# A chunked recurrence with two expert layers: products in pairs of 64 weight columns, and more tiles for px and s0

## The chip, the cores and the metric

The kernel runs on one core of a Trainium2 chip. The metric is device time in microseconds (us) of one execution. In the rows, PE is TensorE's matmuls, PEld its weight loads, DVE VectorE, ACT ScalarE, POOL GpSimd, SP the engine whose queue issues the DMAs. TensorE's clock is granted at one of two levels, 1.2 or 2.4 GHz; the rows give it as a share of 2.4 GHz (0.50 or 1.00, between them a mean over time).

## What is computed

A recurrence over 768 steps for 32 heads (4 batches of 8) with a 40x40 state, then two expert layers on its output:

```
for t in range(S):
    y[:, :, t] = einsum('bhd,bhde->bhe', rt, state)
    Sa = einsum('bhde,bhe->bhd', state, at)
    state = state * wt[:, :, None, :] - einsum('bhd,bhe->bhde', Sa, bt) + einsum('bhd,bhe->bhde', vt, kt)
x = y as (B, S, 320)
x = x + (u * (w_sg @ norm(v) + b_sg)) @ w_out       # u, v = halves of gelu(x @ w_in)
out = (h * sigmoid(conv3(h))) @ w_out2              # h = relu(x @ w_in2)
```

Inputs and outputs are float32.

## The kernel before

**Stages.** `attention` takes the 768 steps in 12 chunks of 64 (`hg`), two chunks to a group (`g`, 6 groups). The 32 heads lie as 16 pairs (`P` is the head of a pair: rows or columns 0 to 63 and 64 to 127); a half `q` of a chunk holds 8 pairs. Then `moe` runs the two layers. The recurrence takes the first 690 us or so, the layers the rest.

**A chunk's work.** `prep` loads the decays and `a`, `k`, `b`, runs two scans on VectorE (`px` and `w`), multiplies `at` by `px` and `kbt` by `w`, and squares `px` and `w` on ScalarE for a guard (`junk`). `products` makes `gk` (L127), masks it into `la`, and transposes `kbt` by TensorE (`pkb`, L133) into `kbn`. `kbt` has one tile, so the next chunk's load waits for the transpositions of this one; `px` and `kbn` have four tiles each, `at` four. `solve_a` inverts a group's triangular blocks on VectorE (60 small operations, L170 and L172, on `mu`); `solve_b` finishes them with 32x32 products (`pn`, `pt`; `n1` shares its tile with `mu`). `chain` is the recurrence proper: `py` (L230), copied to `ys`; `pz` (L237), copied to `vz`; `pS` (L246, L249), the new state, scaled by `px` (L254) and copied to `st`; and, off that path, `pzt` (L258), copied to `zv`. `spart` transposes the state into `s0` (three tiles). `ypart` makes `gh` (L282), masks it into `ghs`, sums `pyo` (L291, L293), multiplies by `px` into `xo` (L296) and stores `xo` with four DMAs.

**Shapes on TensorE.** `a*b` in a row is the part of the array in use: rows times weight columns. Every float32 product is two records in the trace; a transposition by `nc.tensor.transpose` is one. `py`, `pS`, `p0` and `pyo` use 128 rows and 64 weight columns, and two heads of a pair stand in the two halves of the columns; `pz` uses 64*64; `pzt`, `gk`, `gh` and `pkb` 128*128; `pn` and `pt` 32*32.

**What sets the order.** The groups' steps are recorded by the list `ORDER` with priorities (`level`). The framework then fixes each engine's order once, when the program is built, from those priorities, from its own estimates of durations, and from when tiles come free. So a tile more, or a product of another shape, moves instructions on every engine. At run time each engine works through its fixed order and waits where an operand or a tile isn't ready.

Of the kernel before, what the change touches and what calls it, by code (L numbers as in the profile page):

```python
# [10 lines left out]
F32 = mybir.dt.float32  # L11
F16 = mybir.dt.float16
# [3 lines left out]
AF = mybir.ActivationFunctionType  # L16
# [11 lines left out]
def _attention(ctx, tc, ident, gu, wp, wr, a, kb, r, vt, v, x):  # L28
# [5 lines left out]
    nc = tc.nc  # L34
    D, C, J = 40, 64, 4
# [5 lines left out]
    ps_a = ctx.enter_context(tc.tile_pool(name="ps_a", bufs=2, space=PSUM))  # L41
# [24 lines left out]
    las = [const.tile([128, 2, 8, J, C], F32, name=f"la_{i}") for i in range(2)]  # L66
    rys = ring("ys_", 2, [128, 8, 2, C], 0.0, nc.gpsimd)
    rst = ring("st_", 2, [128, 8 * D + 24], 0.0, nc.gpsimd, 8 * D)
    rs0 = ring("s0_", 3, [128, 8 * D + 24], 0.0, nc.gpsimd, 8 * D)
    real = [slice(64 * P, 64 * P + D) for P in range(2)]  # L70
    rq = lambda q: slice(32 * q, 32 * q + 32)
    heads = [(i, P) for i in range(8) for P in range(2)]
    m8 = mask[:, None, None, :].to_broadcast([128, J, 2, C])

    tl, grp = {}, {}

    def flat(t):
        return t.rearrange("p n t -> p (n t)")

    def prep(hg):  # L80

        at = e2.tile([128, 16, 2, C], F32, name="at", bufs=4)
        kbt = e1.tile([128, 16, 2, C], F32, name="kbt")
        px = p4.tile([128, 16, 65], F32, name="px")
        ws = [[], []]
        for q in range(2):
            for i, src in enumerate((wp, wr)):
                t = e2.tile([128, 8, 65], F32, name=f"w{i}")
                nc.sync.dma_start(out=flat(t), in_=src[hg, :, 520 * q:520 * q + 520])
                ws[q].append(t)  # L90
            if q == 0:
                nc.sync.dma_start(out=at.rearrange("p n P t -> p (n P t)"), in_=a[hg])
                nc.sync.dma_start(out=kbt.rearrange("p n c t -> p (n c t)"), in_=kb[hg])
        for q in range(2):
            ns = slice(8 * q, 8 * q + 8)
            w1, w2 = ws[q]
            nc.vector.memset(first[:, :, 0], 1.0)
            nc.vector.tensor_tensor_scan(out=flat(px[:, ns]), data0=flat(w1), data1=flat(first), initial=0.0,
                                         op0=ALU.mult, op1=ALU.add)
            nc.vector.reciprocal(first[:, :, 0], px[:, ns, 64])  # L100
            nc.vector.tensor_tensor_scan(out=flat(w2), data0=flat(w2), data1=flat(first), initial=0.0,
                                         op0=ALU.mult, op1=ALU.add)
            nc.vector.tensor_tensor(out=at[:, ns], in0=at[:, ns], in1=px[:, ns, None, 0:C].to_broadcast([128, 8, 2, C]),
                                    op=ALU.mult)
            nc.vector.tensor_tensor(out=kbt[:, ns], in0=kbt[:, ns],  # L105
                                    in1=w2[:, :, C - 1::-1][:, :, None, :].to_broadcast([128, 8, 2, C]), op=ALU.mult)
            for i, t in enumerate((flat(px[:, ns]), flat(w2))):
                junk = e1.tile([128, 8 * 65], F16, name="junk")
                u = 4 * hg + 2 * q + i
                nc.scalar.activation(out=junk, in_=t, func=AF.Square, scale=2.0 ** -32, accum_out=gu[:, u:u + 1])  # L110
        tl[hg] = dict(px=px, at=at, kbt=kbt)

    def products(hg):

        g, tq = divmod(hg, 2)
        if tq == 0:
            grp[g] = dict(la=las[g % 2])
        la = grp[g]["la"]
        d = tl[hg]
        at, kbt = d["at"], d["kbt"]  # L120
        kbn = p4.tile([128, 32 * D + 24], F32, name="kbn")
        nc.gpsimd.memset(kbn[:, 32 * D:], 0.0)  # L122
        for c in range(4):
            pg = ps_g.tile([128, J, 2, C], F32, name="gk", tag="pg")
            for j in range(J):
                n = 4 * c + j
                nc.tensor.matmul(out=pg[:, j].rearrange("p P t -> p (P t)"),  # L127
                                 lhsT=kbt[:, n].rearrange("p c t -> p (c t)"),
                                 rhs=at[:, n].rearrange("p P t -> p (P t)"), start=True, stop=True)
            nc.vector.tensor_tensor(out=la[:, :, 4 * tq + c].rearrange("p P j t -> p j P t"), in0=pg, in1=m8, op=ALU.mult)  # L130
            pa = ps_a.tile([128, 4, 128], F32, name="pkb", tag="pa")
            for j in range(J):
                nc.tensor.transpose(out=pa[:, j], in_=kbt[:, 4 * c + j].rearrange("p c t -> p (c t)"), identity=ident)  # L133
            nc.scalar.activation(out=kbn[:, 8 * D * c:8 * D * c + 8 * D].rearrange("p (m e) -> p m e", e=D),
                                 in_=pa.rearrange("p j (P e) -> p (j P) e", P=2)[:, :, 0:D], func=AF.Copy)
        cs = slice(4 * tq, 4 * tq + 4)
        for P in range(2):
            rows = rq(2 * P + 1)
            nc.scalar.activation(out=la[rows, P, cs, :, 0:32], in_=la[rows, P, cs, :, 32:64], func=AF.Copy)
        d.update(kbn=kbn)  # L140
# [42 lines left out]
    def solve_b(g, tq):  # L183
# [4 lines left out]
        for c in range(4):  # L188
            for j in range(J):
                for P in range(2):  # L190
                    nc.tensor.matmul(out=pn[rq(2 * P + 1), c, j], lhsT=la[rq(2 * P), P, 4 * tq + c, j, 32:64],
                                     rhs=tn[rq(2 * P), 4 * tq + c, j], start=True, stop=True,
                                     tile_position=(64 * P, 64 * P + 32))
        n1 = e1.tile([128, 4, J, 32], F32, name="n1", tag="mu")
        for P in range(2):
            i1 = rq(2 * P + 1)
            nc.scalar.activation(out=n1[i1], in_=pn[i1], func=AF.Copy)
# [23 lines left out]
    def chain(g, c4):  # L221
# [10 lines left out]
        ys = rys(q)  # L232
# [1 line left out]
            nc.scalar.activation(out=ys[half[P], :, P, 0:D], in_=py[half[P]], func=AF.Copy)  # L234
        pz = ps_c.tile([128, 8, D], F32, name="pz", tag="pc")
        for i, P in heads:
            nc.tensor.matmul(out=pz[half[P], i], lhsT=tt[half[P], 2 * c4 + i // 4, i % 4],  # L237
                             rhs=ys[half[P], i, P, 0:D], start=True, stop=True)
        nc.vector.tensor_copy(vz[half[0], 0, q], pz[half[0]])  # L239
        nc.scalar.activation(out=vz[half[1], 1, q], in_=pz[half[1]], func=AF.Copy)  # L240
        if hg < NH - 1:
# [32 lines left out]
    def ypart(g, c4):  # L274
# [531 lines left out]
```

## Time and profile before

| what | us |
|---|---|
| median of 3 runs (lowest, highest) | 1193.69 (1191.77, 1199.42) |
| the profiled execution | 1188.77 |
| its span, first to last instruction | 1187.1 |
| TensorE busy in the span | 944.4 |
| VectorE busy in the span | 707.7 |

All views are of the one profiled execution. A group of instructions has a busy time (the union of its spans) and the mean length of one record; records of TensorE overlap, so the busy time divided by the count is what one costs in a stream, and the mean length is not. "Idle before" is the time that the engine stood idle just ahead of them, with what ended most of it.

### The profile page before, as it was taken

How to read it: one execution, taken by the hardware profiler on the slowest of the kernel's cores; microseconds unless marked ns; L12 is line 12 of the kernel's file. 1: busy time of each engine (PE TensorE's matmuls, PEld its weight loads, DVE VectorE, ACT ScalarE, POOL GpSimd, SP SyncE). 2: the span in 40 equal slices, each digit the busy share in tenths (PEclk: the TensorE clock that was granted, in tenths of full speed). 3: DMA queues.
4: the chain of work that ended last, by engine and by line, in shares of the span. 5: the costliest groups of instructions: out<-in, count | busy, mean ns of one | idle time of the engine just before them, and what ended most of it. 6: DMA issues, size and time to landing. Idle time of an engine off the chain costs nothing.

```text
span 1187.1 us, 23136 instructions
## 1 busy us (share of the span) xinstructions
PE 944.4 (80%) x9777; PEld 871.2 (73%) x9777; DVE 707.7 (60%) x1325; ACT 468.4 (39%) x913; POOL 145.4 (12%) x164
## 2 busy tenths in 40 slices
PE   3225965797888889789978756899999977999895
PEld 3225864686877778778867745799999966999894
DVE  5693289169692767559233342865556668677763
ACT  2214432433522442352234132423222346777772
POOL 2000000000000000000001012211111424333331
PEclk9655786598766876875876878899999988999997
DMA  9512155225512522420251182000000221000000
GB/s 317 185 36 72 57 174 154 73 84 156 165 60 70 171 104 83 150 64 13 74 177 36 54 240 60 30 1 1 1 1 1 85 60 34 29 23 17 18 23 31
DMA packets 47489, 94.48 MB, mean 80 GB/s; under 512 B 20240, under 2 KB 26384, under 8 KB 44304
## 3 DMA queue, kind: packets, MB, share of 16 engines
q1 hardware_dynamic: 47376, 92.91, 24.8%
q8 instruction: 79, 1.29, 0.5%
q14 instruction: 34, 0.28, 0.1%
HBM read 85.02 MB, written 7.86 MB: 78 GB/s over the span
## 4 chain that ended last, share of the span: by engine, by line
PE 45%; DVE 26%; DMA 8%; ACT 7%; issue 5%; POOL 3%; SPq 1%; DVEq 0%; POOLq 0%; ACTq 0%
PE pv L615 6%; PE pzt L258 4%; DVE mu L172 4%; DVE mtmp L170 4%; PE pr L636 4%; PE gh L282 3%; PE ph L566 3%; PE gk L127 3%; PE pq L706 3%; PE pu L597 3%; DMA raw<-in_moe_w_in 2%; PE pz L237 2%; PE py L230 2%; DMA raw<-in_moe_w_out 2%; DVE mu L163 2%
## 5 line engine op out<-in xcount | busy, mean ns | idle before, releaser
L127 PE MATMUL gk<-at,kbt 128*128 128x128 f32 x384 | 71.5, 353 | 83.9 <-DVE kbt L105 50.5
L127 PEld LDWEIGHTS gk<-at,kbt 128*128 128x128 f32 x384 | 65.3, 260 | 87.1 <-DVE kbt L105 49.5
L692 POOL TENSOR_TENSOR cv<-cv,hz 128x384 f32<-128x384 f32 x64 | 62.4, 984 | 124.2 <-ACT cv L691 124.2
L282 PE MATMUL gh<-r,zv 128*128 128x128 f32 x384 | 72.3, 328 | 1.8 <-DMA r<-in_c_r 1.8
L258 PE MATMUL pzt<-tt,ys 128*128 128x64 f32 x384 | 66.9, 345 | 2.5 <-DVE vz L254 2.5
L258 PEld LDWEIGHTS pzt<-tt,ys 128*128 128x128 f32 x384 | 62.7, 255 | 8.2 <-issue 7.0
L293 PE MATMUL pyo<-ghs,kbn 128*64 128x64 f32 x768 | 60.7, 234 | 7.8 <-DVE ghs L286 7.6
L615 PE MATMUL pv<-sg_hi,vh 128*128 128x384 f32 x192 | 64.5, 336 | 1.2 <-ACT vh L589 1.2
L282 PEld LDWEIGHTS gh<-r,zv 128*128 128x128 f32 x384 | 57.7, 222 | 9.4 <-issue 3.7
L291 PE MATMUL pyo<-r,s 128*64 128x64 f32 x704 | 63.1, 241 | 1.7 <-DVE xo L296 1.7
L615 PE MATMUL pv<-sg_lo,vh 128*128 128x384 f32 x192 | 64.4, 336 | 0.0
L286 DVE TENSOR_TENSOR ghs<-gh,mask 128x512 f32<-128x512 f32 x48 | 32.4, 687 | 52.5 <-PE pyo L293 38.7
L615 PE MATMUL pv<-sg_hi,vl 128*128 128x384 f32 x192 | 63.6, 336 | 0.0
L293 PEld LDWEIGHTS pyo<-ghs,kbn 128*64 128x64 f32 x768 | 52.6, 146 | 14.4 <-DVE ghs L286 9.6
L172 DVE TENSOR_TENSOR mu<-mu,mtmp 128x30 f32<-128x30 f32 (+9 forms) x180 | 59.4, 330 | 5.1
L170 DVE TENSOR_TENSOR mtmp<-mu 128x30 f32<-128x30 f32 (+9 forms) x180 | 59.0, 328 | 5.4
L122 POOL MEMSET kbn<- 128x24 f32 x12 | 1.2, 118 | 497.8 <-PE pyo L293 497.8
L706 PE MATMUL pq<-wv_hi,gh 128*128 128x320 f32 x192 | 43.2, 331 | 22.7 <-ACT gh L695 22.7
L696 DVE TENSOR_TENSOR gl<-cv,gh 128x384 fp32r<-128x384 f32 x64 | 40.9, 640 | 31.8 <-ACT gh L695 31.7
L239 DVE COPY vz<-pz 64x320 f32<-64x320 f32 x24 | 11.6, 481 | 81.0 <-PE pz L237 80.8
L291 PEld LDWEIGHTS pyo<-r,s 128*64 128x64 f32 x704 | 52.2, 147 | 6.4 <-issue 2.8
L230 PE MATMUL py<-vz,la 128*64 128x40 f32 (+1 forms) x768 | 45.6, 290 | 11.8 <-ACT la L209 4.3
(149 smaller groups left out, 2384.7 us busy)
## 6 DMA issues: line engine op xcount, KB each, us to landing
at<-in_c_a SPq DMA_DIRECT2D x12, 1024.0 KB
kbt<-in_c_kb SPq DMA_DIRECT2D x12, 1024.0 KB
zv<-in_c_vt SPq DMA_DIRECT2D x24, 512.0 KB
r<-in_c_r SPq DMA_DIRECT2D x24, 512.0 KB
w<-in_c_wp SPq DMA_DIRECT2D x24, 260.0 KB
w<-in_c_wr SPq DMA_DIRECT2D x24, 260.0 KB
raw<-in_moe_w_in SPq DMA_DIRECT2D x8, 512.0 KB
vz<-in_c_v SPq DMA_DIRECT2D x24, 160.0 KB
```

The source lines that it names most:

```text
L127: nc.tensor.matmul(out=pg[:, j].rearrange("p P t -> p (P t)"), lhsT=kbt[:, n].rearrange("p c t -> p (c t)"), rhs=at[:, n].rearrange("p P t ...
L170: nc.vector.tensor_tensor(out=tv, in0=mu[:, j + 1:32, j:j + 1].to_broadcast([128, n, j]), in1=mu[:, j:j + 1, 0:j].to_broadcast([128, n, j] ...
L172: nc.vector.tensor_tensor(out=mu[:, j + 1:32, 0:j], in0=mu[:, j + 1:32, 0:j], in1=tv, op=ALU.subtract)
L230: nc.tensor.matmul(out=py[half[P], i], lhsT=la[rows, P, 2 * c4 + i // 4, i % 4], rhs=vz[rows, P, q, i], start=True, stop=True)
L258: nc.tensor.matmul(out=pzt[:, i], lhsT=ys[:, i].rearrange("p P e -> p (P e)"), rhs=tt[:, 2 * c4 + i // 4, i % 4], start=True, stop=True)
L282: nc.tensor.matmul(out=gh[:, j].rearrange("p P t -> p (P t)"), lhsT=zv[:, 4 * s + j].rearrange("p c t -> p (c t)"), rhs=r2[:, 4 * s + j].r ...
L291: nc.tensor.matmul(out=pyo[half[P], i], lhsT=s0s[hg, q][:, D * i:D * i + 64], rhs=r2[:, i, P], start=True, stop=False)
L293: nc.tensor.matmul(out=pyo[half[P], i], lhsT=rows_of(kbn, q, i, P), rhs=ghs[:, j, P], start=(hg == 0), stop=True)
L615: nc.tensor.matmul(out=po, lhsT=l[:, fs], rhs=rr[:, k, cs], start=(n == 0), stop=(n == 3 * NT - 1))
L636: nc.tensor.matmul(out=po, lhsT=ww[:, k, ms], rhs=ghl[k][i], start=(n == 0), stop=(n == 3 * NF1 - 1))
L692: nc.gpsimd.tensor_tensor(out=cv, in0=cv, in1=h[:, 1:N2 + 1], op=ALU.mult)
L706: nc.tensor.matmul(out=po, lhsT=gs[k][g][:, ts], rhs=rr[:, k], start=(n == 0), stop=(n == 3 * NF2 - 1))
```

## The change

`pzt` becomes 16 products with 64 weight columns and 128 rows, in the order of the heads, where there were 8 with 128 weight columns; `pz` reads all 128 rows of `tt` and `ys` (the other head's rows of `ys` are zero); `kbn`'s transposition becomes pairs of ordinary products with `kbt` as weights (64 columns) and 80 columns of the identity. `px` gets five tiles, `s0` four; `n1` gets a tile of its own beside `mu`; `ghs` and `xo` share three tiles (they had two each); the squares write into the spent `w` tile and `junk` goes.

```
-    rs0 = ring("s0_", 3, [128, 8 * D + 24], 0.0, nc.gpsimd, 8 * D)
+    rs0 = ring("s0_", 4, [128, 8 * D + 24], 0.0, nc.gpsimd, 8 * D)
+    id80 = ident.rearrange("p (P e) -> p P e", P=2)[:, :, 0:D]
-        px = p4.tile([128, 16, 65], F32, name="px")
+        px = p4.tile([128, 16, 65], F32, name="px", bufs=5)
-                junk = e1.tile([128, 8 * 65], F16, name="junk")
-                nc.scalar.activation(out=junk, in_=t, func=AF.Square, scale=2.0 ** -32, accum_out=gu[:, u:u + 1])
+                nc.scalar.activation(out=flat(w1), in_=t, func=AF.Square, scale=2.0 ** -32, accum_out=gu[:, u:u + 1])
-            pa = ps_a.tile([128, 4, 128], F32, name="pkb", tag="pa")
+            pa = ps_a.tile([128, J, 2, D], F32, name="pkb", tag="pa")
             for j in range(J):
-                nc.tensor.transpose(out=pa[:, j], in_=kbt[:, 4 * c + j].rearrange("p c t -> p (c t)"), identity=ident)
+                for h in range(2):
+                    nc.tensor.matmul(out=pa[half[h], j], lhsT=kbt[:, 4 * c + j, h], rhs=id80, start=True, stop=True)
-        n1 = e1.tile([128, 4, J, 32], F32, name="n1", tag="mu")
+        n1 = e1.tile([128, 4, J, 32], F32, name="n1")
         for i, P in heads:
-            nc.tensor.matmul(out=pz[half[P], i], lhsT=tt[half[P], 2 * c4 + i // 4, i % 4],
-                             rhs=ys[half[P], i, P, 0:D], start=True, stop=True)
+            nc.tensor.matmul(out=pz[half[P], i], lhsT=tt[:, 2 * c4 + i // 4, i % 4],
+                             rhs=ys[:, i, P, 0:D], start=True, stop=True)
-        for i in range(8):
-            nc.tensor.matmul(out=pzt[:, i], lhsT=ys[:, i].rearrange("p P e -> p (P e)"),
-                             rhs=tt[:, 2 * c4 + i // 4, i % 4], start=True, stop=True)
+        for i, P in heads:
+            nc.tensor.matmul(out=pzt[half[P], i], lhsT=ys[:, i, P], rhs=tt[:, 2 * c4 + i // 4, i % 4],
+                             start=True, stop=True)
-            ghs = p2.tile([128, J, 2, C], F32, name="ghs")
+            ghs = p3.tile([128, J, 2, C], F32, name="ghs", tag="gx")
-        xo = p2.tile([128, 2, J, C], F32, name="xo")
+        xo = p3.tile([128, 2, J, C], F32, name="xo", tag="gx")
```

VectorE, where a group ends (the solve of the next one is done, `ypart` stores its results): this is the order before, in group 3.

```order
L296 TENSOR_TENSOR xo<-pyo,px 128x512 x2
L98 SCALAR_TENSOR_TENSOR px<-w_2961,first 128x520
L100 RECIPROCAL first<-px 128x8
L103 TENSOR_TENSOR at<-at,px 128x1024
L101 SCALAR_TENSOR_TENSOR w_2963<-w_2963,first 128x520
L105 TENSOR_TENSOR kbt<-kbt,w_2963 128x1024
L97 MEMSET first 128x8
```

VectorE with the change, at the start of a group, just after the next solve's first transpositions:

```order
L297 TENSOR_TENSOR xo<-pyo,px 128x512
L164 STREAM_TRANSPOSE mu<-la_103 64x1024 x2
L99 SCALAR_TENSOR_TENSOR px<-w_4175,first 128x520
L171 TENSOR_TENSOR mtmp<-mu 128x30
L101 RECIPROCAL first<-px 128x8
L104 TENSOR_TENSOR at<-at,px 128x1024
```

The scan of `px` now stands inside the solve. VectorE with the change, at the end of that group, for the same chunk:

```order
L179 STREAM_TRANSPOSE tt_99<-mu 128x32x32
L287 TENSOR_TENSOR ghs<-gh,mask 128x512
L240 COPY vz<-pz 64x320
L106 TENSOR_TENSOR kbt<-kbt,w_4177 128x1024
L106 TENSOR_TENSOR kbt<-kbt,w_4183 128x1024
```

The scans, the reciprocals and the multiplications of `at` moved some 75 rows ahead, into the solve; of the chain behind `xo` only the multiplications of `kbt` are left at the group's end.

TensorE, in a pair of `chain` steps, before (the number behind a name is a buffer's):

```order
L237 MATMUL pz<-ys_105,tt_100 64x40 x15
L258 MATMUL pzt<-tt_100,ys_105 128x64 x8
L133 MATMUL pkb<-ident,kbt 128x128 x4
L203 MATMUL pt<-tt_100,n_3505 32x32
L249 MATMUL pS<-vz,kbn 64x40
L230 MATMUL py<-vz,la_104 64x40 x16
L249 MATMUL pS<-vz,kbn 64x40 x15
L133 MATMUL pkb<-ident,kbt 128x128 x2
L237 MATMUL pz<-ys_106,tt_100 64x40
```

TensorE at the same place with the change:

```order
L238 MATMUL pz<-ys_105,tt_99 64x40 x16
L247 MATMUL pS<-st_109,ident 64x320 x2
L259 MATMUL pzt<-tt_99,ys_105 64x64 x13
L250 MATMUL pS<-vz,kbn 64x40
L259 MATMUL pzt<-tt_99,ys_105 64x64 x3
L134 MATMUL pkb<-ident,kbt 64x80 x2
L231 MATMUL py<-vz,la_103 64x40 x16
L250 MATMUL pS<-vz,kbn 64x40 x15
L134 MATMUL pkb<-ident,kbt 64x80 x5
```

All rows here are of one array shape, where four alternated; `pzt` and `pkb` stand in smaller pieces between the others. Over TensorE's whole order the array's shape changes 306 times with the change, 331 times before.

VectorE in the first solve (`run(solve_a(0))`), before:

```order
L172 TENSOR_TENSOR mu<-mu,mtmp 128x26x5
L170 TENSOR_TENSOR mtmp<-mu 128x150
L172 TENSOR_TENSOR mu<-mu,mtmp 128x25x6
L170 TENSOR_TENSOR mtmp<-mu 128x168
L172 TENSOR_TENSOR mu<-mu,mtmp 128x24x7
```

VectorE at the same place with the change, where the fifth `px` tile is first used:

```order
L171 TENSOR_TENSOR mtmp<-mu 128x150
L99 SCALAR_TENSOR_TENSOR px<-w_1067,first 128x520
L173 TENSOR_TENSOR mu<-mu,mtmp 128x25x6
L101 RECIPROCAL first<-px 128x8
L171 TENSOR_TENSOR mtmp<-mu 128x168
```

A scan and a reciprocal of the fifth chunk now stand inside the first solve.

## Rows read from the trace of the kernel before

**Rows 1.** Windows by stage: prologue, recurrence, layers; columns stand in its first line.

```profile
core 0: us, PE busy (x) PEld busy (x) DVE busy (x) ACT busy (x) POOL busy (x), PEclk, DMA share, GB/s
0.00:100.00 100.00, 25.54 (x224) 23.97 (x224) 71.30 (x125) 21.70 (x51) 7.56 (x22) 0.70 0.48 160
100.00:690.00 590.00, 482.08 (x7152) 430.92 (x7152) 332.54 (x627) 211.38 (x404) 9.20 (x14) 0.73 0.33 103
690.00:1187.10 497.10, 436.79 (x2401) 416.29 (x2401) 303.90 (x573) 235.32 (x460) 128.62 (x128) 0.94 0.12 36
```

**Rows 2.** TensorE's waits, 100 to 690 us: total, times, longest.

```profile
PE gk L127 <- DVE first L97: 19.8, 3, 7.6
PE pt L203 <- ACT n L197: 16.6, 13, 4.7
PE gk L127 <- issue: 13.2, 2, 7.0
PE pyo L293 <- DVE ghs L286: 7.6, 9, 3.5
...
PE gk L127 <- DVE kbt L105: 5.4, 5, 2.7
PE pS L249 <- DVE vz L239: 4.8, 5, 1.6
```

**Rows 3.** Timeline of VectorE ahead of one such wait: start, us, operation, idle.

```profile
382.27 1.29 DVE L296 TENSOR_TENSOR xo<-pyo,px 128x512 f32<-128x512 f32 x2 [3.76 <-PE pyo L293]
383.59 1.24 DVE L98 TENSOR_TENSOR_SCAN px<-w,first 128x520 f32<-128x520 f32 x1
384.87 0.21 DVE L100 RECIPROCAL first<-px 128x8 f32<-128x8 f32 x1
384.99 1.18 DVE L103 TENSOR_TENSOR at<-at,px 128x1024 f32<-128x1024 f32 x1
386.08 1.23 DVE L101 TENSOR_TENSOR_SCAN w<-w,first 128x520 f32<-128x520 f32 x1
387.35 1.22 DVE L105 TENSOR_TENSOR kbt<-kbt,w 128x1024 f32<-128x1024 f32 x1
```

**Rows 4.** Timeline of TensorE at the end of it.

```profile
388.63 2.08 PE L127 MATMUL gk<-at,kbt 128*128 128x128 f32 x8 [6.05 <-DVE first L97]
```

**Rows 5.** Groups by shape, 100 to 690 us: array*columns, count, busy, mean ns, idle.

```profile
L258 PE MATMUL pzt<-tt,ys 128*128 128x64 f32 x384 | 66.9, 345 | 2.5 <-DVE vz L254 2.5
L291 PE MATMUL pyo<-r,s 128*64 128x64 f32 x704 | 63.1, 241 | 1.7 <-DVE xo L296 1.7
L293 PE MATMUL pyo<-ghs,kbn 128*64 128x64 f32 x768 | 60.7, 234 | 7.8 <-DVE ghs L286 7.6
L293 PEld LDWEIGHTS pyo<-ghs,kbn 128*64 128x64 f32 x768 | 52.6, 146 | 14.4 <-DVE ghs L286 9.6 <-issue 1.4 <-DVE mu L172 0.2
L237 PE MATMUL pz<-ys,tt 64*64 64x40 f32 x768 | 43.8, 270 | 0.4 <-ACT ys L234 0.4
L230 PE MATMUL py<-vz,la 128*64 128x40 f32 x704 | 42.3, 293 | 10.7 <-ACT la L209 4.3 <-DVE first L100 3.4 <-ACT vz L240 3.1
```

**Rows 6.** The same view over the whole span, transpositions.

```profile
L133 PE MATMUL pkb<-ident,kbt 128*128 128x128 f32 x192 | 40.8, 344 | 0.8 <-ACT kbn L134 0.8
```

**Rows 7.** Timeline, runs of one product at 1.2 GHz: pzt, pkb, py.

```profile
426.45 3.67 PE L258 MATMUL pzt<-tt,ys 128*128 128x64 f32 x16
429.92 1.06 PE L133 MATMUL pkb<-ident,kbt 128*128 128x128 f32 x4
...
362.87 1.88 PE L230 MATMUL py<-vz,la 128*64 128x40 f32 x32
```

**Rows 8.** Timeline, runs of one product at 2.4 GHz: pkb, gh, pyo, pzt, py.

```profile
154.51 0.60 PE L133 MATMUL pkb<-ident,kbt 128*128 128x128 f32 x4
154.94 1.95 PE L282 MATMUL gh<-r,zv 128*128 128x128 f32 x16
156.82 0.69 PE L293 MATMUL pyo<-ghs,kbn 128*64 128x64 f32 x16
160.00 1.38 PE L293 MATMUL pyo<-ghs,kbn 128*64 128x64 f32 x32 [1.41 <-DVE ghs L286]
...
239.89 2.00 PE L258 MATMUL pzt<-tt,ys 128*128 128x64 f32 x16
...
470.52 1.13 PE L230 MATMUL py<-vz,la 128*64 128x40 f32 x32
```

**Rows 9.** Timeline, shapes alternating at 2.4 GHz.

```profile
501.10 0.33 PE L291 MATMUL pyo<-r,s 128*64 128x64 f32 x2
501.36 0.49 PE L282 MATMUL gh<-r,zv 128*128 128x128 f32 x2
501.78 0.33 PE L293 MATMUL pyo<-ghs,kbn 128*64 128x64 f32 x2
```

**Rows 10.** Windows: one with gk, gh and pkb, one mixed, two of chain steps.

```profile
148.00:162.00 14.00, 11.80 (x165) 11.13 (x167) 10.02 (x14) 4.68 (x11) 0.00 (x0) 1.00 0.56 189
236.00:274.00 38.00, 34.59 (x666) 30.50 (x664) 27.09 (x62) 14.79 (x31) 0.12 (x1) 0.99 0.33 107
333.00:353.00 20.00, 18.70 (x195) 16.34 (x196) 18.45 (x48) 4.50 (x10) 0.00 (x0) 0.50 0.21 70
357.00:377.00 20.00, 20.00 (x218) 17.46 (x216) 2.84 (x5) 3.41 (x7) 0.00 (x0) 0.50 0.09 28
```

**Rows 11.** Chain of waits, two DMAs: start, us, what.

```profile
140.05 4.70 DMA kbt<-in_c_kb
269.26 4.24 DMA x_attn<-xo
```

**Rows 12.** SP's waits, 100 to 690 us.

```profile
SPq L93 <- PE pkb L133: 35.3, 8, 14.3
```

**Rows 13.** SP's issues of the stores: min/median/max ns of an issue, first and last.

```profile
L301 SPq DMA_DIRECT2D x_attn<-xo x96: 286/363/1317, 162.1 to 683.1; - x96
```

More of the change, by code (lines that the diff above doesn't have):

```diff
@@ L120, in products @@
         at, kbt = d["at"], d["kbt"]
-        kbn = p4.tile([128, 32 * D + 24], F32, name="kbn")
+        kbn = p4.tile([128, 32 * D + 24], F32, name="kbn", bufs=4)
         nc.gpsimd.memset(kbn[:, 32 * D:], 0.0)
@@ L130, in products @@
             nc.vector.tensor_tensor(out=la[:, :, 4 * tq + c].rearrange("p P j t -> p j P t"), in0=pg, in1=m8, op=ALU.mult)
-            pa = ps_a.tile([128, 4, 128], F32, name="pkb", tag="pa")
+            pa = ps_a.tile([128, J, 2, D], F32, name="pkb", tag="pa")
             for j in range(J):
-                nc.tensor.transpose(out=pa[:, j], in_=kbt[:, 4 * c + j].rearrange("p c t -> p (c t)"), identity=ident)
-            nc.scalar.activation(out=kbn[:, 8 * D * c:8 * D * c + 8 * D].rearrange("p (m e) -> p m e", e=D),
-                                 in_=pa.rearrange("p j (P e) -> p (j P) e", P=2)[:, :, 0:D], func=AF.Copy)
+                for h in range(2):
+                    nc.tensor.matmul(out=pa[half[h], j], lhsT=kbt[:, 4 * c + j, h], rhs=id80, start=True, stop=True)
+            nc.scalar.activation(out=kbn[:, 8 * D * c:8 * D * c + 8 * D],
+                                 in_=pa.rearrange("p j P e -> p (j P e)"), func=AF.Copy)
         cs = slice(4 * tq, 4 * tq + 4)
```

## Prediction, written before the changed kernel was run

> **What bounds the kernel now.** I read the windows by stage first. The layers' stage holds TensorE at 437 of 497 us with a granted clock of 0.94, and the change touches none of its lines; so I leave it as it is, moved to wherever the recurrence ends. In the recurrence's 590 us TensorE is busy 482, VectorE 333, ScalarE 211 [rows 1]: TensorE sets the pace, with 108 us of idle time. The list of its waits says what for [rows 2]. The largest are five waits of `gk`, 19.8 and 13.2 us together 33.0, and five short ones of 5.4. The timeline of VectorE ahead of one of the five shows its making [rows 3]: two `xo` end, and only then five operations of `prep` run one after the other, from 383.59 to 388.57, because the scan's `px` tile is the one that `xo` has just read. TensorE has worked off its queue and stands still for 6.05 us until `gk` starts [rows 4]. Next come the costs of the products in a stream [rows 5 to 8]: a run of 16 `pzt` records takes 3.67 us at 1.2 GHz and 2.00 at 2.4, although it moves only 64 columns; `gh` with 128 moving columns takes 1.95 for 16, so `pzt` pays for its 128 weight columns. 16 `pyo` records, with 64 weight columns, two halves in turn and 64 moving columns, take 0.69 [rows 8].
>
> **pzt.** It now has `pyo`'s form of [rows 8]: 32 records for the same work. At 2.4 GHz I take 1.38 for them (the run of 32), at 1.2 GHz 1.88 (the run of 32 `py`, 40 moving columns, the nearest at that clock [rows 7]). The 24 runs cost 66.9 us [rows 5], 2.79 each, which lies 47% of the way from 2.00 to 3.67. So: 0.53 x 1.38 + 0.47 x 1.88 = 1.62 each, 38.8 in all, a gain of 28.1. Bounds: `py`'s price at both clocks (1.13 and 1.88) gives 35.5, a gain of 31.4; no overlap of the halves at all is bounded by the mixed `pyo` groups, (63.1 + 60.7) / 1472 = 84 ns a record [rows 5], 768 x 84 = 64.6, a gain of 2.3.
>
> **pkb.** Four transpositions take 0.60 at 2.4 GHz and 1.06 at 1.2 [rows 7, 8]; the 48 fours cost 40.8 [rows 6], 0.85 each, 54% at the lower clock. Now eight products make 16 records with 80 moving columns. The nearest row is the 16 `pyo`, 0.69; by columns 0.86; between them 0.78, and at the lower clock by `pkb`'s own ratio 1.37. So 0.46 x 0.78 + 0.54 x 1.37 = 1.10 against 0.85: 12 us lost. Bounds: 0.69 and 1.22 lose 6; 84 ns x 80/64 a record, one after the other, would be 80.6 us, 40 lost.
>
> **pz.** From 64*64 to 128*64 it takes `py`'s form: 42.3/704 = 60.1 ns a record against 43.8/768 = 57.0 [rows 5], times 768: 2.4 lost. The two `py` halves share all 128 rows of the array, and yet 32 records follow each other in 1.13 us [rows 8], 35 ns apart, though one weight load of this width alone has a mean length of 146 [rows 5]: loads for one half run beside the other half's work. A rule speaks against that: the Trainium skill (TensorE: Matmul & The Clock Gate, Part 3, What overlaps and what doesn't) has a weight load overlap a running matmul only where the row groups differ. By it the new pairs, all over 128 rows, would load and multiply by turns, and the time would be that of the last rival; the trace does not agree, with `py` at 60 ns a record beside `pz`'s 57.
>
> **Changes of shape.** Alternating, two `pyo` and two `gh` records take 0.68 us from one `pyo` to the next (501.10 to 501.78) [rows 9]; in runs they cost 2 x 0.043 and 2 x 0.122, together 0.33 [rows 8]. Two changes cost 0.35, one 0.18. The built order has 331 changes before and 306 now: 25 x 0.18 = 4.5 gained.
>
> TensorE's work thus falls by 28.1 - 12 - 2.4 + 4.5 = 18.2 us. I count it in full, since with the waits gone little but TensorE's queue is left.
>
> **The fifth px tile.** In the order, the scans, reciprocals and `at` multiplications stand in the solve, ahead of the stores; behind them only `kbt`'s 1.22 us [rows 3] remains before `gk`. I leave 1.5 us of each of the five waits: 33.0 - 7.5 = 25.5 gained. VectorE has the room (333 of 590 us). What is late next is `kbt` itself: one tile, whose load (4.70 us [rows 11]) starts when the last `pkb` of the chunk before is done, and SP already stands 35.3 us for that [rows 12]. Between that `pkb` and the next `gk` the order has 33 to 60 `pyo`, at two records of 84 ns 5.5 to 10 us; load and multiplication want 5.9. So I count nothing, with up to 2.5 us ten times, 25, as the bound.
>
> **The prologue.** One scan (1.24) and one reciprocal (0.21 [rows 3]) of the fifth chunk now stand inside the first solve, which TensorE waits for: 1.4 lost.
>
> **The smaller edits.** `s0`'s fourth and `n1`'s own tile can only release waits; among TensorE's longest waits none is theirs, so zero. The squares into `w` hold that tile some 1 us longer; its next load comes a chunk later: zero. `ghs` and `xo` have three tiles for four: as built, 13 of 23 `xo` take the tile of the `xo` before them and so wait for its stores (4.24 us to landing and four issues of 0.36 [rows 11, 13]). Between two stand the masks and 64 `pyo` records, 5.4 us at 84 ns. I count zero; the bound is in the second-last rival.
>
> **The sum.** 18.2 + 25.5 - 1.4 = 42.3 us gained on the profiled execution of 1188.8: 1146.5. That execution lies 4.9 under the median of the runs; I add it back and forecast **1151**. By the bounds above (`pzt` 2.3 to 31.4 gained, `pkb` 6 to 40 lost, `kbt` up to 25 lost) the likely case reaches from 1132 to 1178.
>
> **Rivals.** (1) *The clock rises.* In 20 us windows of chain steps TensorE was busy 18.7 and 20.0 and was granted 0.50; in one with `gk`, `gh` and `pkb`, 1.00 [rows 10]. The mean of 0.73 puts 54% of the recurrence, 319 us, at 1.2 GHz. Denser chain steps could be granted 2.4: if a fifth of that time is, 32 us more go: 1119. For it: the stretch from 236 to 274 us, with chain steps in it too, was granted 0.99. Against it: in both windows at 0.50 TensorE was busy nearly all the time, so filling its waits need not raise the clock. (2) *The gain comes back as waits.* `pzt` and `pkb` fill TensorE's queue while `vz` goes through VectorE. With 1.9 instead of 3.67 us of it, `pS`, which now waits 4.8 us in all [rows 2], may wait 0.7 more in each of 24 steps, 17; with `kbt`'s 25 the gain is gone: 1151 + 42 = 1193. (3) *Slower: xo in its neighbour's tile.* VectorE works in order; an `xo` that waits for a landing holds up the masks of `gh` and `gk` behind it. With nothing to cover it a wait is 4.24 and four issues of 0.36, 5.7 us; 13 of them make 74, and the kernel 1151 + 74 = 1225. It decides from 42/13 = 3.3 us a wait upwards; for it speaks that stores stand in SP's queue behind loads that wait, against it the 5.4 us of `pyo`. (4) *The halves run singly.* `pzt` gains 2.3 and `pkb` loses 40: TensorE's work grows by 35.4 instead of falling by 18.2, which makes 1151 + 54 = 1205.
>
> **Chances.** My forecast 0.52, (1) 0.18, (2) 0.18, (3) 0.08, (4) 0.04. The range 1105 to 1195 holds the first three but for some of their tails, and leaves out (3) and (4). A difference of 1%, 12 us, is about what a measurement of this kernel can tell from none. Faster by more: the forecast, (1) and a quarter of (2), 0.75; within it: most of (2) and half of (4), 0.15; slower: (3), the other half of (4) and a tail of (2), 0.10.
>
> **What the changed profile would show.** `pzt` at about 39 us busy for 768 records and runs of 32 in 1.4 to 1.9; `pkb` at about 53 for 768; `pz` near 46. The waits of `gk` on `prep` down from 33 to under 10. Wrong would be: a wait of `gk` on `kbt` of over 10 us in all, or of `xo` on the stores; `pS` waiting over 15; weight loads and matmuls of `pzt` by turns. A granted clock over 0.78 in the recurrence means (1).

## The result, and the profile after

The changed kernel takes 1147.51 us (median of 4 runs, 1141.21 to 1148.20) against 1192.73 for the kernel before on the same chip (4 runs): ratio 0.960, 95% interval 0.955 to 0.966. The forecast was 1151. The profiled execution of the changed kernel took 1147.78, with a span of 1146.1.

The number was right; the way to it was right only in part. First the windows by stage of the changed kernel, columns as in [rows 1], the recurrence cut at its last `pyo`:

```profile
100.00:641.00 541.00, 423.23 (x8016) 381.41 (x8016) 328.07 (x620) 208.79 (x398) 9.64 (x14) 0.79 0.35 109
649.00:1146.10 497.10, 437.89 (x2401) 417.20 (x2401) 304.84 (x576) 235.01 (x461) 127.93 (x128) 0.94 0.12 36
```

and the kernel before, cut in the same way:

```profile
100.00:680.00 580.00, 481.81 (x7151) 430.79 (x7152) 331.12 (x622) 210.93 (x401) 9.20 (x14) 0.73 0.32 102
```

The layers' stage is the same, 437.9 us of TensorE's time in 497. The recurrence is 39 us shorter. TensorE's busy time in it fell by 58.6, three times the 18.2 that were predicted, and its idle time did not fall by 25 but rose from 98 to 118. The granted clock rose from 0.73 to 0.79.

The two can be told apart by a rough sum. Of a mean clock c, (1 - c)/0.5 is the share of time at 1.2 GHz: 54% before, 42% after. A run of 16 `pzt` took 3.67 us there and 2.00 at 2.4 GHz [rows 7, 8], so a busy microsecond at 1.2 GHz holds 0.455 us more than the same work needs at 2.4. Busy time x (1 - 0.455 x share) is then TensorE's work at full clock (it takes busy time to be spread over both clocks as all time is): 363 before, 342 after. Of the 58.6 us, 21 are work and 38 are clock. Split by the clock that the trace gives for each moment, without that assumption, 267 of the 482 busy us stand at 1.2 GHz before and 177 of the 423 after, and the same 0.455 gives 360 and 343: 17 of work and 41 of clock. The rough sum stands for every kernel in the table below.

The waits of TensorE, 100 to 650 us of the changed kernel, answer to [rows 2]:

```profile
PE pn L192 <- DVE tn L177: 19.4, 1, 19.4
PE pn L192 <- DVE xo L297: 15.0, 6, 4.2
PE pS L250 <- DVE vz L240: 13.5, 7, 4.0
PE pz L238 <- ACT tt L209: 10.7, 4, 3.7
PE gk L127 <- DVE kbt L106: 10.7, 3, 6.4
PE pS L247 <- DVE vz L255: 7.3, 2, 4.5
PE pt L204 <- ACT n L198: 7.2, 8, 3.6
...
PE gk L127 <- DVE ghs L287: 3.2, 2, 2.7
```

`gk`'s waits on `prep` (33.0) are gone from the list; in their place `pn` waits for the solve and for `xo`, and `pS` for `vz`. How `xo` comes into it is seen on VectorE's timeline, columns as in [rows 3]:

```profile
386.83 1.23 DVE L99 TENSOR_TENSOR_SCAN px<-w,first 128x520 f32<-128x520 f32 x1
...
393.21 1.23 DVE L102 TENSOR_TENSOR_SCAN w<-w,first 128x520 f32<-128x520 f32 x1
394.36 0.67 DVE L297 TENSOR_TENSOR xo<-pyo,px 128x512 f32<-128x512 f32 x1
```

and on TensorE's:

```profile
395.08 1.92 PE L192 MATMUL pn<-tn,la 32*32 32x32 f32 x64 [4.20 <-DVE xo L297]
```

With a fifth `px` tile the scans need no `xo` ahead of them, so two blocks of `prep` now run before `xo`. But `xo` reads `pyo`, whose PSUM tile is one of the two that `pn` and `pkb` use too, so `pn` waits.

The groups by shape, 100 to 641 us, answer to [rows 5, 6]:

```profile
L259 PE MATMUL pzt<-tt,ys 128*64 128x64 f32 x768 | 41.1, 257 | 0.0
L134 PE MATMUL pkb<-ident,kbt 128*64 128x80 f32 x640 | 39.7, 260 | 3.7 <-ACT kbn L135 3.7
L238 PE MATMUL pz<-ys,tt 128*64 128x40 f32 x768 | 35.6, 257 | 16.4 <-ACT tt L209 10.7 <-ACT ys L235 5.7
L231 PE MATMUL py<-vz,la 128*64 128x40 f32 x704 | 32.5, 251 | 5.1 <-ACT la L210 3.8 <-ACT zv L262 0.8 <-ACT vz L241 0.3
```

`py`, whose form nobody touched, is the gauge: it fell from 42.3 to 32.5 for the same 704 records, by the clock alone: at either clock its records follow each other as before, 31 and 54 ns apart at 2.4 and 1.2 GHz, 30 and 54 now. Next to it `pzt` (66.9 to 41.1) gained by its form, and `pz` (43.8 to 35.6) mostly by the clock (32 and 57 ns apart before, 29 and 53 now).

### The profile page after: what moved, and what is told of

Its sections match the earlier page's. It is cut to its first block, busy times and chain, and to the rows that moved or that the text cites. A ratio compares the mean times of both kernels' runs of the same rounds, so it can differ in the third digit from the quotient of the medians.

```text
span 1146.1 us, 25040 instructions
## 1 busy us (share of the span) xinstructions
PE 889.3 (78%) x10737; PEld 823.9 (72%) x10737; DVE 706.4 (62%) x1325; ACT 468.3 (41%) x913; POOL 145.4 (13%) x165
## 3 DMA queue, kind: packets, MB, share of 16 engines
q1 hardware_dynamic: 47376, 92.91, 25.8%
## 4 chain that ended last, share of the span: by engine, by line
PE 37%; DVE 31%; DMA 14%; ACT 8%; issue 5%; POOL 3%; SPq 1%; DVEq 0%; POOLq 0%; ACTq 0%
PE pv L616 6%; DVE mu L173 4%; DVE mtmp L171 4%; PE pr L637 3%; PE gh L283 3%; PE gk L127 3%; PE pq L707 3%; DMA raw<-in_moe_w_out 3%; PE pu L598 3%; DMA kbt<-in_c_kb 3%; PE ph L567 2%; DVE px L99 2%; DVE w L102 2%; DMA raw<-in_moe_w_in 2%; POOL cv L693 2%
## 5 line engine op out<-in xcount | busy, mean ns | idle before, releaser
L127 PE MATMUL gk<-at,kbt 128*128 128x128 f32 x384 | 67.7, 329 | 55.8 <-DVE kbt L106 52.5
L127 PEld LDWEIGHTS gk<-at,kbt 128*128 128x128 f32 x384 | 57.4, 229 | 60.2 <-DVE kbt L106 53.3
L192 PE MATMUL pn<-tn,la 32*32 32x32 f32 x768 | 23.7, 225 | 61.8 <-DVE tn L177 46.6
L192 PEld LDWEIGHTS pn<-tn,la 32*32 32x32 f32 x768 | 20.5, 138 | 64.3 <-issue 27.3
L283 PE MATMUL gh<-r,zv 128*128 128x128 f32 x384 | 63.5, 312 | 1.9 <-ACT wi_hi L480 1.6
L292 PE MATMUL pyo<-r,s 128*64 128x64 f32 x704 | 60.7, 244 | 3.1 <-DVE xo L297 3.1
L283 PEld LDWEIGHTS gh<-r,zv 128*128 128x128 f32 x384 | 53.2, 213 | 5.9 <-ACT wi_hi L480 1.8
L688 DVE SCALAR_TENSOR_TENSOR cv<-hz,cw,cv 128x384 f32<-128x384 f32 x64 | 41.3, 650 | 23.0 <-ACT cv L687 23.0
L623 ACT ACTIVATE gh<-g 128x384 fp32r<-128x384 f32 x32 | 16.8, 524 | 90.6 <-POOL g L620 90.6
L707 PEld LDWEIGHTS pq<-wv_hi,gh 128*128 128x128 f32 x192 | 32.9, 196 | 27.9 <-ACT gh L696 27.9
```

What stands on the lines that cost most here:

```text
L292: nc.tensor.matmul(out=pyo[half[P], i], lhsT=s0s[hg, q][:, D * i:D * i + 64], rhs=r2[:, i, P], start=True, stop=False)
L688: nc.vector.scalar_tensor_tensor(out=cv, in0=h[:, 1:N2 + 1], scalar=cw[:, 1, f:f + 1], in1=cv, op0=ALU.mult, op1=ALU.add)
L707: nc.tensor.matmul(out=po, lhsT=gs[k][g][:, ts], rhs=rr[:, k], start=(n == 0), stop=(n == 3 * NF2 - 1))
```

## The experiments

All ran beside the kernel before, each with 4 runs of its own; ratios are to that kernel on the same chip. "Work" is the sum above. Window, busy and clock are those of the profiled execution, from 100 us to its last `pyo`; most of the rows follow in the text. Three cautions go with them. The runs came in four rounds, in which the kernel before took 1186 to 1193 us, so windows of different rounds can differ by some 7 us for that alone; the ratios take this out. The work column reads 353 to 363 for the four kernels with all three products in their old forms, so a difference of under 10 us in it says little by itself. And a row is one execution; the mean clock of the whole span, over all runs of a kernel, bears its order out: 0.82 before, 0.83 in e23, 0.84 in e2 and e13, 0.85 in the changed kernel, e5, e12 and e19, 0.86 in e1, e4 and e16, 0.87 in e3 and e18, 0.88 in e11.

| kernel | ratio (95%) | window, us | busy | idle | clock | work |
|---|---|---|---|---|---|---|
| before | 1 | 580 | 482 | 98 | 0.73 | 363 |
| changed | 0.960 (0.955-0.966) | 541 | 423 | 118 | 0.79 | 342 |
| e1: three forms alone | 0.968 (0.964-0.972) | 545 | 410 | 135 | 0.82 | 343 |
| e2: tiles alone | 0.970 (0.965-0.975) | 551 | 457 | 94 | 0.77 | 361 |
| e13: before, fifth px | 0.982 (0.976-0.988) | 560 | 442 | 118 | 0.78 | 353 |
| e23: before, n1 apart | 0.983 (0.978-0.988) | 560 | 461 | 99 | 0.76 | 360 |
| e5: changed, old pzt | 0.982 (0.975-0.989) | 555 | 450 | 105 | 0.80 | 369 |
| e12: changed, prep not raised | 0.970 (0.965-0.976) | 548 | 424 | 124 | 0.79 | 343 |
| e4: changed, old pkb | 0.956 (0.952-0.960) | 521 | 403 | 118 | 0.81 | 333 |
| e3: changed, four px | 0.950 (0.947-0.954) | 522 | 406 | 116 | 0.82 | 340 |
| e11: old pkb and four px | 0.923 (0.918-0.928) | 496 | 383 | 113 | 0.85 | 330 |
| e16: e11, n1 in mu's tile | 0.937 (0.932-0.942) | 510 | 390 | 120 | 0.84 | 333 |
| e18: e11, old pz | 0.935 (0.930-0.940) | 504 | 400 | 104 | 0.83 | 338 |
| e19: e11, ghs and xo apart | 0.958 (0.952-0.963) | 518 | 400 | 118 | 0.81 | 331 |

**The two halves of the change.** e1 takes the three new forms into the kernel before; e2 leaves the changed kernel's tiles and undoes the three forms:

```
e1:  pzt, pz, pkb as in the changed kernel; px 4, s0 3, n1 in mu's tile, junk, ghs and xo apart
e2:  px 5, s0 4, n1 apart, gx shared, no junk; pzt, pz, pkb as before
```

> The kernel before with the three product forms of the change alone (pzt, pz and pkb in pairs of 64 weight columns); every tile count as before. Theory A, the forms bring the gain, by pzt's price and by a higher granted clock: 35 to 45 us off, 1148 to 1158, clock in the recurrence 0.78 or more, the five waits of gk on prep still there (about 33). Theory B, the fifth px tile brings most of it, as the prediction had it (25.5 of 42): 18 us off, about 1175, clock as before (0.73).

> The change's tile edits alone (px, s0, n1, ghs and xo, the squares into w), with the three products in their old forms. Theory A: 0 to 10 us off, 1183 to 1193, clock 0.73, the waits of gk on prep gone and others in their place. Theory B: 25 us off, about 1168.

e1 measured 1150.08 (1147.48 to 1153.26), e2 1154.12 (1146.23 to 1157.56), beside 1185.97. The windows, of e1:

```profile
100.00:645.00 545.00, 409.80 (x8016) 370.27 (x8016) 331.15 (x622) 211.18 (x401) 9.34 (x14) 0.82 0.34 108
```

and of e2:

```profile
100.00:651.00 551.00, 457.03 (x7148) 408.35 (x7149) 329.18 (x620) 207.80 (x395) 9.21 (x14) 0.77 0.33 107
```

Each half gains 3%; both together gain 4%, not 6. The forms alone take 20 us of work away and raise the clock by more than the whole change does, and half of the 72 us that TensorE is less busy returns as idle time (98 to 135). The tiles alone leave the work (361) and hardly touch the idle time (94): the 25 us of busy time that go are clock.

**px back to four tiles.**

```
-        px = p4.tile([128, 16, 65], F32, name="px", bufs=5)
+        px = p4.tile([128, 16, 65], F32, name="px")
```

> The changed kernel with four px tiles again. Theory A: within 8 us of the changed kernel, 1147 to 1156. Theory B: the five waits of gk come back, 25 us: about 1172.

1127.83 (1126.92 to 1128.45): faster than the changed kernel, whose interval it does not touch. The edit that was to bring 25.5 of the 42.3 us costs 1% where it was made.

```profile
100.00:622.00 522.00, 406.32 (x7968) 364.39 (x7966) 330.44 (x622) 206.66 (x396) 9.35 (x14) 0.82 0.36 113
```

TensorE's waits of this run, 100 to 650 us:

```profile
PE gk L127 <- DVE first L98: 22.5, 5, 7.0
PE gk L127 <- issue: 16.1, 3, 8.0
...
PE pn L192 <- DVE xo L297: 3.9, 5, 0.8
...
PE pn L192 <- DVE tn L177: 2.9, 1, 2.9
```

`gk` waits 38.6 us on `prep` again, more than before, and `pn` no longer waits on `xo` and `tn` (34.4 in the changed kernel, 6.8 here). The idle time is the same, 116 for 118: the fifth tile only exchanged the one for the other. Of the 19 us between the windows (12 by the two ratios) 17 are busy time, nearly all by the clock.

**pkb as transpositions again** (the `pkb` lines of the diff undone, with them the copy into `kbn`, which the new form writes in one piece).

> The changed kernel with pkb as four transpositions of 128 columns again; pzt and pz stay in pairs. If the clock rose because of pkb's new form, it falls to about 0.75 in the recurrence and the time rises by 10 to 20, to 1157 to 1167. If it rose because of pzt, the clock stays near 0.79 and the time falls by the 5 us that pkb's pairs cost more, less the added changes of shape: 1143 to 1148.

1134.07 (1129.97 to 1135.94): by the intervals of the ratios not to be told from the changed kernel.

```profile
100.00:621.00 521.00, 402.61 (x7536) 363.48 (x7536) 328.16 (x621) 208.12 (x397) 9.33 (x14) 0.81 0.35 113
```

The work falls by 9, the clock does not fall: `pkb`'s new form costs about what the prediction said, and isn't what raised the clock.

**Both undone.**

> The changed kernel with four px tiles and with pkb as four transpositions, both undone together. If the two undone parts act on different things (TensorE's work, which pkb's new form raised by some 10 us at full clock, and the order of VectorE's work, which the fifth px tile upset), they add: 1128 (four px tiles alone) less 10 to 13, so about 1116, ratio 0.94. Rival: what is gained by either is the same idle and slow-clock time, so that it can be gained once only: 1123 to 1132, ratio 0.945 to 0.955. TensorE busy in the recurrence should fall by 10 us against the run with four px tiles if its clock stays at 0.82.

1099.26 (1097.95 to 1101.20), beside 1191.82.

```profile
100.00:596.00 496.00, 382.52 (x7508) 345.11 (x7502) 329.38 (x623) 206.83 (x397) 9.34 (x14) 0.85 0.38 119
```

It is faster than both theories had it: 0.923 is below the sum of the two gains (0.94). TensorE's busy time fell by 24 against e3 where 10 were expected, since the clock did not stay at 0.82. Against e4, which differs by the fifth `px` tile alone, 20 of 25 us are busy time at nearly equal work. This is the fastest kernel of the study, 4% ahead of the changed one by the two ratios.

**The old pzt in the changed kernel.**

> The changed kernel with pzt in its old form, 128 weight columns and 24 runs of 16 records. By the price in the prediction pzt's old form costs 28 us more of TensorE's work at a mean clock like before's, 24 at the clock of now: 1140 + 24 = 1164 on this chip, ratio 0.98. Theory of the clock: the slow form also holds TensorE at 1.2 GHz, so the granted clock of the recurrence falls from 0.79 to 0.75 or lower and more than 28 us are lost, ratio 0.985 or above. Rival: in the changed kernel TensorE's idle time covers part of it, and less than 12 us are lost: ratio 0.97 or below.

1165.48 (1160.67 to 1174.94): (0.982 - 0.960) x 1191.8 = 26 us are lost (11 to 40 by the two intervals), so the 24 expected are met, and the theory that this form holds the clock down isn't borne out: the clock is 0.80. Its window, and its group by shape in it:

```profile
100.00:655.00 555.00, 450.47 (x7630) 403.04 (x7630) 328.69 (x620) 207.26 (x396) 9.23 (x14) 0.80 0.34 107
```

```profile
L259 PE MATMUL pzt<-tt,ys 128*128 128x64 f32 x384 | 65.3, 337 | 5.8 <-DVE vz L255 5.8
```

65.3 busy for 41.1 with the new form at nearly the same clock: 24.2.

**prep of later chunks without a raised priority.**

```
-                    with level(2): prep(2 * g + 4 + int(it[1]))
+                    prep(2 * g + 4 + int(it[1]))
```

> The changed kernel, five px tiles kept, with prep of chunks 4 on emitted without a raised priority, so that VectorE takes an xo ahead of prep's operations where both are ready. Theory: the fifth px tile let prep run ahead of xo, which holds pyo's PSUM tile and with it pn; then pn's waits on xo (15.0 us) fall under 6 and the time comes near that with four px tiles: 1128 to 1135. Rival: not the order on VectorE but the earlier loads and kbt's single tile cost the time, and the order hardly moves: waits of pn on xo stay over 10, time within 1% of the changed kernel's 1140 (ratio 0.955 to 0.965).

1154.48 (1154.19 to 1156.16), by the ratios 1% slower than the changed kernel, with intervals that just overlap. `pn`'s waits on `xo` fell from 15.0 to 8.6, between what the theory (under 6) and its rival (over 10) had, but `pt` waited 11.4 for 7.2, `gk` on `kbt` 12.5 for 10.7, and `pz` on `ys` 11.2 for 5.7:

```profile
PE pn L192 <- DVE tn L177: 17.4, 1, 17.4
PE gk L127 <- DVE kbt L106: 12.5, 4, 6.5
PE pt L204 <- ACT n L198: 11.4, 8, 3.2
PE pz L238 <- ACT ys L235: 11.2, 3, 4.7
...
PE pn L192 <- DVE xo L297: 8.6, 4, 2.7
```

So almost halving `pn`'s wait on `xo` was worth nothing; that this wait is the price of the fifth tile isn't borne out, though no run with five tiles took all of it away.

**The fifth px tile alone, on the kernel before** (the `px` line, and the squares into `w`, which makes the room).

> The kernel before with a fifth px tile and nothing else but what makes room for it (the squares are written into w instead of a tile of their own). By the prediction's largest term gk's waits on prep (33 us) all but go and the time falls by 25: 1161 on this chip, ratio 0.978. Theory after the first runs: prep comes ahead of xo, and pn and others wait instead: gk's waits go, but the idle time of TensorE in the recurrence (98 us) falls by less than 10, and what is gained, if anything, is clock: 1175 to 1190. Rival: it is slower than before by over 1%, since the old forms leave TensorE no slack.

1167.97 (1165.72 to 1172.55), 21 us (1.8%) gained, close to the 25 of the prediction and below both later theories.

```profile
100.00:660.00 560.00, 441.67 (x7146) 395.58 (x7143) 323.05 (x620) 206.43 (x395) 9.25 (x14) 0.78 0.34 105
```

But it isn't the gain that was predicted. `gk`'s waits on `prep` go, and TensorE is idle longer, 118 us for 98. The first of its waits, 100 to 660 us:

```profile
PE pn L190 <- DVE tn L175: 38.4, 5, 24.8
PE pt L202 <- ACT n L196: 14.2, 12, 3.4
PE gh L281 <- DMA r<-in_c_r: 10.6, 4, 3.7
```

`prep` inside the solve makes the solve longer: the third takes 58 us from its first transposition (253.4) to `tn` (311.6), where it took 43 before (247.9 to 290.7), and `pn` waits 38.4 us for the solves (6.1 before). What falls is TensorE's busy time, by 40 us, at a clock of 0.78 for 0.73.

**n1 apart from mu.** The prediction counted it at nothing. On the kernel before, by itself:

```
-        n1 = e1.tile([128, 4, J, 32], F32, name="n1", tag="mu")
+        n1 = e1.tile([128, 4, J, 32], F32, name="n1")
```

> The kernel before with n1 in a tile of its own and nothing else. By the prediction: nothing, ratio 0.995 to 1.005. Theory: the next solve no longer waits for n1, tn of the second group ends at some 240 us instead of 293, VectorE is free later in each group for prep and the masks, and TensorE's waits of gk and pt (33 and 17 us) shrink: ratio 0.975 to 0.99. Rival: the solve comes earlier, but then stands in the way of the chain's own work on VectorE: vz and ghs come later, ratio 1.0 to 1.01.

1168.55 (1166.90 to 1170.47), beside 1187.87: 1.7% gained. The other way round, from the fastest kernel:

> The fastest kernel so far (the changed one with four px tiles and pkb as transpositions, ratio 0.923) with n1 put back into mu's tile. Theory: n1's own tile is worth most of the 2% by which the run with the three forms alone (ratio 0.968) stands behind that with four px tiles (0.950), because n1 in mu's tile lets the next solve begin only when n1 has been read: the second group's tn then ends near 290 us instead of 231, and the ratio is 0.937 to 0.945. Rival: the gain is that of the other small edits, the prediction's zero for n1 holds, and the ratio stays between 0.918 and 0.928.

1114.33 (1112.77 to 1117.56): 1.5% lost by the two ratios, at the edge of what the theory gave. The start of the third solve (the first is `run(solve_a(0))`) shows the mechanism; the columns are the shortest, median and longest operation, then the first and last start. Before, from 200 to 300 us:

```profile
L163 DVE STREAM_TRANSPOSE mu<-la x2: 1947/1948/1948, 247.9 to 249.9; 64x1024 f32<-64x1024 f32 x2
```

With `n1` apart (e23), and in the fastest kernel:

```profile
L163 DVE STREAM_TRANSPOSE mu<-la x2: 1906/1918/1929, 211.8 to 213.8; 64x1024 f32<-64x1024 f32 x2
```

```profile
L163 DVE STREAM_TRANSPOSE mu<-la x2: 1903/1906/1909, 201.1 to 203.1; 64x1024 f32<-64x1024 f32 x2
```

In `mu`'s tile, `n1` keeps the next solve from starting until the products of this one have read it: 37 us after the second solve's `tn` (209.1 to 211.0); without that it starts as soon as that solve is done. The theory of e23 was wrong on what follows from it: `gk` on `prep` still waits 31.2 us there (33.0 before), `pt` on the copy of `n1` 16.4 (16.6 [rows 2]), and the idle time is 99 for 98. What is gained is busy time, 21 us, at equal work. The windows of e23 and of e16:

```profile
100.00:660.00 560.00, 460.79 (x7144) 412.64 (x7146) 333.87 (x622) 209.84 (x400) 9.22 (x14) 0.76 0.33 105
```

```profile
100.00:610.00 510.00, 389.84 (x7534) 352.31 (x7534) 326.02 (x622) 208.74 (x398) 9.33 (x14) 0.84 0.36 116
```

**pz over 64 rows again, in the fastest kernel.**

> The fastest kernel so far (ratio 0.923) with pz over 64 rows again. The prediction had pz's new form 2.4 us dearer: then this is faster by 2 us, ratio 0.921, not to be told from none. By the spacings of the records in the traces (57 and 32 ns before, 53 and 29 now, at 1.2 and 2.4 GHz) it is 2 us slower, ratio 0.925. If new pairs over 128 rows loaded and multiplied by turns, undoing them would gain over 20 us: below 0.91. Anything above 0.93 or with pz's share unchanged would again be the order of the work and the clock, not pz's own price.

1110.48 (1109.19 to 1114.41), 1.3% slower than the fastest by the two ratios, more than its own price.

```profile
100.00:604.00 504.00, 400.39 (x7520) 357.02 (x7516) 331.19 (x622) 207.72 (x397) 9.19 (x14) 0.83 0.37 117
```

Its own group there, and that of the fastest kernel:

```profile
L237 PE MATMUL pz<-ys,tt 64*64 64x40 f32 x768 | 40.2, 257 | 8.7 <-ACT ys L234 8.7
```

```profile
L237 PE MATMUL pz<-ys,tt 128*64 128x40 f32 x768 | 35.1, 251 | 8.6 <-ACT ys L234 8.2 <-ACT tt L208 0.4
```

5.1 us dearer, part of it by the lower clock (0.83 for 0.85). The new pairs don't load and multiply by turns.

**ghs and xo in two tiles each again, in the fastest kernel.**

```
-            ghs = p3.tile([128, J, 2, C], F32, name="ghs", tag="gx")
+            ghs = p2.tile([128, J, 2, C], F32, name="ghs")
-        xo = p3.tile([128, 2, J, C], F32, name="xo", tag="gx")
+        xo = p2.tile([128, 2, J, C], F32, name="xo")
```

> The fastest kernel so far (ratio 0.923) with ghs and xo in two tiles each again instead of three for both. The prediction priced the shared tiles at nothing: ratio 0.918 to 0.928. Its rival, an xo or a mask that waits for the stores of the xo before it, would make the kernel faster here, by 5 us or more: below 0.918. Theory from the first runs: any edit that changes the order of the work on VectorE moves the time by some per cent, through TensorE's granted clock; then it is slower, above 0.928, with more time at 1.2 GHz in the recurrence.

1136.93 (1133.60 to 1141.62): 3.7% slower, although it only gives back tiles.

```profile
100.00:618.00 518.00, 400.27 (x7490) 362.63 (x7486) 333.31 (x623) 206.23 (x396) 9.35 (x14) 0.81 0.35 114
```

The work is that of the fastest kernel (331 for 330), the idle time 5 us more, the busy time 18 more. TensorE waits less for `ghs` and `xo` than in the fastest kernel, 7 us for 19, so these waits aren't the loss; that it is the order and the clock is what is left, and isn't shown by itself.

## Why the prediction was right in its number, and where its steps were wrong

- **What bounds the kernel.** Right for the layers' stage, which did not move, and too simple for the recurrence. The idle time was read as something that a released wait gives back; in all 14 kernels of the table it stays between 94 and 135 us, whatever waits were taken out. TensorE is not alone on the path. The chain of work that ended last, as a share of the whole span, before and after:

```profile
PE 45%; DVE 26%; DMA 8%; ACT 7%; issue 5%; POOL 3%; SPq 1%; DVEq 0%; POOLq 0%; ACTq 0%
PE 37%; DVE 31%; DMA 14%; ACT 8%; issue 5%; POOL 3%; SPq 1%; DVEq 0%; POOLq 0%; ACTq 0%
```

  Of this chain, the part from 100 us to the last `pyo` holds 306 us of TensorE before and 219 after, 169 and 199 of VectorE, 35 and 53 of DMAs, 28 and 34 of ScalarE, 39 and 31 of issue. Of the 87 us that TensorE gave up, 54 came back on the other three. That VectorE is busy only 333 of 590 us, which the prediction read as room, says nothing of this; in the fastest kernel (e11) VectorE holds the largest part of the chain there, 218 of 496 us, TensorE 177.
- **TensorE's work, -18.2.** Right: 17 to 21 by the two sums above, 20 for the forms alone (e1). `pzt` gave 24.2 (e5) for 28.1, within its bounds; `pkb` cost about 9 (e4, and again between e3 and e11) for 12. No run takes the changes of shape (4.5) by themselves. `pz` is the wrong sign, though small: 35.6 busy where 46 were expected, most of that by the clock. The prediction weighed the Trainium skill (TensorE: Matmul & The Clock Gate, Part 3, What overlaps and what doesn't), by which loads overlap only where row groups differ. The trace after does not agree either: `pz`'s records over all 128 rows follow each other at 29 ns at 2.4 GHz and 53 at 1.2, over 64 rows at 32 and 57, and undoing the form (e18) gained nothing.
- **The fifth px tile, -25.5.** This step failed. It took `gk`'s waits for TensorE's loss and priced what comes behind them at `kbt` alone. `gk`'s waits did go, and `kbt` came next as said (10.7 us), but other waits came in their place: `pn` for `xo` (15.0; 3.9 with four tiles, e3) and for `tn` (19.4; 2.9 in e3), `pS` for `vz` (20.8; 6.2 in e3, but 18.9 in e1 with four tiles too, so it isn't the tile's alone). On the kernel before the tile gains 1.8% (e13), with 20 us more idle time; in the changed kernel it loses 1% (e3), and 3.6% where `pkb` is undone as well (e4 against e11).
- **The prologue, +1.4.** Not seen: the first solve's `tn` starts at 93.2 us with the change, at 95.0 before. The cost came at later solves and wasn't counted: in e13 the waits for their ends grew by 32 us. In the changed kernel the second solve's `tn` is no later either (206.8 for 209.1; 205.9 with four tiles, e3); TensorE reaches it earlier and stands 19.4 us.
- **The smaller edits, 0.** Wrong for `n1` (1.7% and 1.5%) and for the shared tiles of `ghs` and `xo` (3.7%, and not by TensorE's waits for them). The rule used, that an edit whose wait is not in TensorE's list is worth nothing, overlooks that a tile fixes when another engine may start, and so the whole order; for `n1` the start of the solve shows it, for the shared tiles it is argued.
- **Rivals.** Both (1) and (2) came true together. The clock passed its sign (0.79, over 0.78) and took 38 us off TensorE's busy time; the gain came back as waits by both its signs, `pS` over 15 and `gk` on `kbt` over 10. TensorE's busy time fell by 40 us more than the sum had (58.6 for 18.2), by the clock; its idle time ended 44 above the sum's (24 forecast to go, 20 added). That the two errors cancelled to within 4 us is luck. (3) did not happen: VectorE's idle time ahead of `xo` is put down to `pyo` alone, and none of it to the stores, in the changed kernel's groups, and undoing the shared tiles lost time (e19):

```profile
L297 DVE TENSOR_TENSOR xo<-pyo,px 128x512 f32<-128x512 f32 x24 | 16.4, 683 | 54.8 <-PE pyo L294 54.8
```

  (4) did not happen either (`pzt` and `pz` above).
- **The range.** The likely case, 1132 to 1178, isn't what its bounds add up to: `pzt` and `pkb` at their best give 1151 - 3.3 - 6 = 1142, and all three at their worst 1151 + 25.8 + 28 + 25 = 1230. The result lies within either.
- **Left open.** What sets the granted clock. Two windows of the changed kernel:

```profile
418.00:445.00 27.00, 21.05 (x342) 19.06 (x339) 25.07 (x68) 10.22 (x24) 0.00 (x0) 0.50 0.12 35
456.00:489.00 33.00, 28.06 (x559) 25.66 (x557) 17.67 (x27) 11.71 (x27) 0.12 (x1) 1.00 0.55 174
```

  The first holds chain steps with `pkb`, `pt` and `p0`; the second has `pyo`, `gh` and `gk` among them. Before, chain steps alone were granted 0.50 at 18.7 of 20 us busy [rows 10]. Every edit that changes the order changes what such a stretch holds; but no run here changed that alone, so nothing on the cause is shown. Nor is what the clock is worth on the path: in seven executions of the kernel before on one chip the span went from 1189.5 us at a mean clock of 0.809 to 1180.5 at 0.833, 9 us, less than the sum of busy time would give (about 20). Over seven runs on each of three chips, 0.01 of clock goes with 3.0 to 3.6 us. By that estimate the changed kernel's 0.03 would be worth some 10 of its 45 us, and the 0.02 of e13 some 7 of its 21. So "clock" above is a share of TensorE's busy time; part of it can come back as idle time, and that the clock is what makes a kernel faster isn't shown.

## What to carry to other kernels

Price the work of the busiest engine by rows of the same form and expect that to hold; don't count a removed wait as time gained until the order says what that engine would wait for next, and don't price at zero an edit that lets another engine start a long block earlier. Where the framework sets the order from the tiles, and the granted clock moves with every such edit, the parts of a change don't add: try it without each of its parts, for here undoing two of them (one priced rightly as a loss, one wrongly as a large gain) was worth as much again as the whole change.

## What was not expected of the hardware

- The granted clock changed TensorE's busy time by more than the work did (38 to 41 us for 17 to 21). Between kernels with equal work, e4 and e11 or e11 and e19, TensorE's busy time differs by 18 to 20 us, at mean clocks of 0.81 and 0.85.
- Two column halves over all 128 rows run no less densely than over 64 (`pz`: 29 ns a record at 2.4 GHz for 32), and 32 records of `pkb` with 80 moving columns take 1.33 us at 2.4 GHz:

```profile
385.74 1.33 PE L134 MATMUL pkb<-ident,kbt 128*64 128x80 f32 x32 [0.75 <-ACT kbn L135]
```
